# Swapped query halves and a 72-column transpose of the diagonal block

## The chip, the core and the metric

The kernel runs on one core of one Trainium2 chip. The metric is the device time of one execution in microseconds (us). Times of single instructions are given in nanoseconds (ns). TensorE does the matrix products and, by a product with an identity, the transposes; VectorE (DVE), ScalarE (ACT) and GpSimd (POOL) do elementwise work; SyncE (SP) issues the DMAs.

## What is computed

```python
def _attn_ref(q, k, v, s):                      # q, k, v: 4 x 8 x 576 x 64, s: 4 x 8 x 576
    scores = scale * np.matmul(q, k.transpose(0, 1, 3, 2))
    causal = np.triu(np.ones((S, S), dtype=bool), k=1)
    cum = np.cumsum(np.maximum(s, 0.0), axis=-1)
    bias = -(cum[:, :, :, None] - cum[:, :, None, :])
    scores = np.where(causal, -1000000000.0, scores + np.minimum(bias, 0.0))
    attn = softmax(scores)                       # with 1e-9 added to the sum
    return np.matmul(attn, v)

def _moe_ref(x, domain_probs, w1, w2):           # x: 2304 x 512, w1: 4 x 512 x 1024, w2: 4 x 1024 x 512
    p = domain_probs / (domain_probs.sum(-1, keepdims=True) + 1e-09)
    for e in range(4):
        out += p[:, e:e + 1] * (np.maximum(x @ w1[e], 0.0) @ w2[e])
```

The attention of 32 heads is causal; its output, with the heads side by side, goes through a mixture of four experts.

## The kernel before

The program has two stages. In the first, some 270 us long, the attention is computed head by head, and the first expert's products on row groups (lines 945 and 960) are put between as filling for TensorE. In the second, products of the other experts run back to back (line 1302).

**Visits and tiles.** The first eight heads are visited twice with float32 products (lines 745 and 844), the other 24 once, in visits that the code calls `joint`. A joint visit has four tiles of 128 query rows, m = 1 to 4; tile m holds the query rows from 128m - 64 to 128m + 63 (`rows(m)`). The keys lie in blocks of 128. So a tile's rows meet m + 1 key blocks, and its last block, the diagonal one, has entries above zero for the second half of the tile's rows alone: its keys begin at 128m, and the causal mask takes the first 64 rows away.

**A tile's way.** TensorE writes scores into a PSUM bank `S` (line 748, two products with 128 and 68 rows of weights). VectorE adds the mask, takes the extreme and writes the tile `a` to SBUF (line 759, `mask`). ScalarE takes the exponential (767), the sum is inverted (773, 775), the tile is scaled (line 461, called from 780). TensorE transposes the tile block by block into a PSUM bank `T` (line 794); the bank is evicted as a high part on ScalarE (line 466) and a low part on VectorE (line 823). Last come the products with V (line 844). For a key block n those use only query columns from 128n on, so of the diagonal block's transpose only the last 64 columns are used.

**The transpose.** In `nc.tensor.transpose(out, in_, identity)` the tile's block (128 rows by 128 key columns) is the stationary operand that is loaded as weights, and the identity is what is moved, with as many columns as rows come out transposed. There are 456 of them: 336 in the joint visits (2 + 3 + 4 + 5 blocks in each of 24), and 96 of these are of diagonal blocks.

**Order.** Each step is a task with engines, a cost and a priority. A planner, `Sched.run`, walks a model of time and gives each engine its instructions in the order in which the model frees them. All DMAs go through SP's one queue, in that order. The bias parts of the scores come from a DRAM array `ce_d`, written by `emit_ced` (lines 525 to 528) at about 50 us, and read by each joint visit's key and query DMAs (lines 706 to 715) and by `pair_rows` (line 587).

Of the kernel before, what the change touches and what calls it, by code (L numbers as in the profile page):

```python
# [11 lines left out]
F32 = mybir.dt.float32  # L12
F32R = mybir.dt.float32r
AF = mybir.ActivationFunctionType
ALU = mybir.AluOpType
# [38 lines left out]

def rows(m):
    return (0, 64) if m == 0 else (128 * m - 64, 128 * m + 64)
# [48 lines left out]
T_LAG = 200  # L105
S_LAG = 50
# [229 lines left out]
def body(ctx, tc, qk, qkv0, vp, s, dp, w1, w1s, w2, w2s, out):  # L336
# [13 lines left out]
    idn = apool.tile([P, P], F32, name="idn")  # L350
    mask = apool.tile([P, 448 + P], F32, name="mask")
# [88 lines left out]
    ce_d = dram.tile([BH, 6, S], F32R, name="ce_d")  # L440
# [48 lines left out]
    for _ in range(NWARM):  # L489
        nc.tensor.matmul(mo[1], ones_bf[:, 0:128], ones_bf, start=True, stop=True)  # L490
# [5 lines left out]
    make_identity(nc, idn)  # L496
    nc.gpsimd.memset(mask, 0.0)
    nc.gpsimd.affine_select(out=mask[:, 448:], in_=mask[:, 448:], pattern=[[-1, P]], base=0, channel_multiplier=1, compare_op=ALU.is_ge, fill=-8e9)
# [36 lines left out]
    t_ced = sch.add({"SP": 1500}, emit_ced, [t_clo], prio=T_CE, give=[("KK", "ce")], xfer=6 * BH * S * 4)  # L535
# [13 lines left out]
    def emit_mask0(e):  # L549
        hi(e, mask0, mask[:, 448:])  # L550
        nc.gpsimd.memset(mask0[64:P, 0:64], -8e9)
# [8 lines left out]
    def pair_rows(j, h, base):  # L560
# [24 lines left out]
        def f(e):  # L585
            for x, c in ((384, 0), (0, 2)):
                nc.sync.dma_start(out=pair_tile(k)[0:4, x:x + P].bitcast(F32).rearrange("p (y n) -> p y n", y=2),
                                  in_=ced[h - 1:h + 1, c:c + 4, 0:64].rearrange("y r n -> r y n"))
# [28 lines left out]
        tt = sch.add({"PE": t_pe(P)}, lambda e: nc.tensor.transpose(tok["T", (k, "p")][:, 0:P], tok["a0", k], idn), [nm], prio=pr - PT,  # L617
# [36 lines left out]
    for j, (h, ms) in enumerate(VISITS):  # L654
# [40 lines left out]
        else:  # L695
            if pq:
                qk_ready = [ld, ldc]
            else:
# [7 lines left out]
                def f(e, j=j, h=h, ext=ext):  # L706
                    nc.sync.dma_start(out=tok["KK", j][0:64, :, 0:ext].bitcast(F32), in_=AB(j)[64:128, 0:1, 0:ext].bitcast(F32).to_broadcast([64, 2, ext]))
                    nc.sync.dma_start(out=tok["KK", j][64:128, 0, 0:ext].bitcast(F32), in_=AB(j)[64:128, 1, 0:ext].bitcast(F32))
                    nc.sync.dma_start(out=tok["KK", j][64:68, 1, 0:ext].bitcast(F32), in_=ced[h, 2:6, 0:ext])
# [6 lines left out]
                qk_ready = [k_dma, q_dma]  # L716
# [12 lines left out]
        for m in ms[1:] if joint else ms:  # L729
# [7 lines left out]
            for pi, (j0, j1) in enumerate(pieces):  # L737
# [18 lines left out]
                def f(e, m=m, n=n, a=a, j0=j0, j1=j1, c=c, pi=pi):  # L756
                    mx = tok["mx", c]
                    z = tok[f"a{m}", c]
                    nc.vector.tensor_tensor_reduce(  # L759
                        out=z[0:n, j0:j1], in0=tok["S", (c, pi)][0:n, 0:j1 - j0], in1=mask[0:n, 448 - a + j0:448 - a + j1], scale=-0.125,  # L760
# [24 lines left out]
            for pi, blocks in enumerate(tp):  # L785
# [4 lines left out]
                def f(e, m=m, j=j, blocks=blocks, c=c, pi=pi, first=first):  # L790
# [226 lines left out]
    sch.watch = cx_users + [t_ced, t_chi, t_clo, t_cum3]  # L1017
# [521 lines left out]
```

## Time and profile before

| | before |
|---|---|
| time, median of 3 runs | 914.52 us (914.31 to 915.73) |
| profiled execution, time | 914.74 us |
| profiled execution, span | 913.0 us |
| TensorE busy | 905.0 us, 99% of the span |
| VectorE, ScalarE, GpSimd busy | 77%, 55%, 55% |
| granted TensorE clock, mean | 0.999 |

The span reaches from the first to the last instruction; 1.74 us of the profiled execution lie around it. A matmul's recorded time is longer than the pace at which matmuls follow each other, since they are pipelined: the pace is read from one start to the next, and where the engine changes from one kind of product to another, over a few of them.

### The profile page before, as it was taken

The page shows a single profiled execution, that of the slowest core. Times are in us where ns is not written, and L with a number is a line of the kernel's source. Part 1 is how long each engine was busy: PE and PEld are TensorE (multiplying, and loading weights), DVE is VectorE, ACT ScalarE, POOL GpSimd, SP SyncE. Part 2 cuts the span into 40 slices and gives each one's busy share as a digit, 9 for nine tenths or more (in the row PEclk, how much of TensorE's full clock was granted, in tenths as well). Part 3 has the DMA queues.
Part 4 walks back from the last instruction along what each step waited for, and adds up shares of the span by engine and source line. Part 5 has one row for each costly group of instructions (what it writes and reads, how often), then busy time and mean ns, then how long its engine had stood idle before and what let it go on. Part 6 is the DMA issues. An engine that isn't in the chain of part 4 may idle for free.

```text
span 913.0 us, 16499 instructions
## 1 busy us (share of the span) xinstructions
PE 905.0 (99%) x5566; PEld 879.2 (96%) x5566; DVE 705.6 (77%) x1599; ACT 501.3 (55%) x1129; POOL 506.4 (55%) x528
## 2 busy tenths in 40 slices
PE   9999999999999999999999999999999999999998
PEld 6789999899999999999999999999999999999998
DVE  6878787888861854888787788788877887787886
ACT  6898999999972334435343533444244534444343
POOL 4688787887744891055344624471366317451655
PEclk9999999999999999999999999999999999999999
DMA  6788887879626996984786468746775667756201
GB/s 165 197 246 236 225 229 219 250 194 255 181 94 221 392 382 239 357 286 173 264 286 207 161 219 303 243 158 218 252 260 200 204 215 253 256 205 220 70 18 69
DMA packets 101279, 201.34 MB, mean 221 GB/s; under 512 B 11256, under 2 KB 66620, under 8 KB 101196
## 3 DMA queue, kind: packets, MB, share of 16 engines
q1 hardware_dynamic: 101196, 200.30, 67.2%
q8 instruction: 44, 0.72, 0.3%
q14 instruction: 39, 0.32, 0.1%
HBM read 157.34 MB, written 29.05 MB: 204 GB/s over the span
## 4 chain that ended last, share of the span: by engine, by line
PE 91%; ACT 4%; DVE 2%; POOL 1%; issue 1%; DMA 1%; SPq 0%; ACTq 0%; POOLq 0%
PE pb L1302 52%; PE mo L1302 9%; PE mo L945 6%; PE mo L960 5%; PE pv L844 4%; PE pb L960 3%; PE T L794 3%; PE S L748 2%; PE pb L945 2%; PE S L745 2%; ACT a L767 1%; PE X L794 1%; ACT aTh L466 1%; DMA AB_r<-AB_r 1%; DVE aTl L823 1%
## 5 line engine op out<-in xcount | busy, mean ns | idle before, releaser
L1302 PE MATMUL pb<-x,w1h 128*128 128x384 f32 x1064 | 270.7, 335 | 0.0
L1302 PEld LDWEIGHTS pb<-x,w1h 128*128 128x128 f32 x1064 | 191.5, 188 | 2.0 <-ACT t L1335 1.5
L1302 PE MATMUL pb<-x,w1l 128*128 128x384 f32 x532 | 177.8, 334 | 0.0
L1310 ACT ACTIVATE pb<-pb 128x384 f32<-128x384 f32 x112 | 53.2, 475 | 200.5 <-DVE t L1342 111.8
L453 POOL TENSOR_TENSOR hT_r<-t,hT_r 128x768 fp32r<-128x768 f32 x18 | 34.3, 1903 | 167.8 <-PE pb L1302 139.4
L1302 PE MATMUL pb<-hT_r,w2h 128*128 128x384 f32 x432 | 109.7, 334 | 0.0
L1302 PEld LDWEIGHTS pb<-x,w1l 128*128 128x128 f32 x532 | 99.9, 188 | 0.0
L466 ACT ACTIVATE hT_r<-t 128x768 fp32r<-128x768 f32 x76 | 64.0, 843 | 47.3 <-PE pb L1302 44.3
L767 ACT ACTIVATE a<-a,mx 128x576 f32<-128x576 f32 (+4 forms) x136 | 81.0, 597 | 12.8 <-DVE mx L759 9.6
L1425 DVE TENSOR_TENSOR acc<-pb,acc 128x384 f32<-128x384 f32 x152 | 78.5, 549 | 9.6 <-ACT pb L1310 6.1
L945 PE MATMUL mo<-xg,w1h 128*128 128x384 f32 (+1 forms) x304 | 78.3, 327 | 0.0
L1302 PEld LDWEIGHTS pb<-hT_r,w2h 128*128 128x128 f32 x432 | 78.0, 188 | 0.0
L453 DVE TENSOR_TENSOR hT_r<-t,hT_r 128x768 fp32r<-128x768 f32 x58 | 59.8, 1031 | 23.2 <-ACT hT_r L466 22.7
L461 POOL TENSOR_SCALAR a<-a,sm 128x576 f32<-128x576 f32 (+5 forms) x111 | 60.5, 552 | 28.6 <-DVE sm L775 15.0
L1302 PE MATMUL pb<-xg,w2h 128*128 128x384 f32 x288 | 73.3, 335 | 0.0
L1302 PE MATMUL pb<-hT_r,w2l 128*128 128x384 f32 x216 | 72.2, 334 | 0.0
L1342 DVE TENSOR_TENSOR t<-pb,t 128x384 f32<-128x384 f32 x78 | 39.8, 551 | 38.5 <-ACT t L1335 25.6
L453 POOL TENSOR_TENSOR xg<-t,xg 128x768 fp32r<-128x768 f32 x19 | 42.9, 2259 | 40.8 <-ACT xg L466 40.8
L1070 DVE TENSOR_TENSOR t<-t 128x768 f32<-128x768 f32 (+1 forms) x42 | 65.1, 1555 | 0.1
L823 DVE TENSOR_TENSOR aTl<-T,aTh 128x256 fp32r<-128x256 f32 (+2 forms) x103 | 51.2, 508 | 4.6 <-ACT aTh L466 3.5
L759 DVE CUSTOM_DVE_ANT_0 a<-S,mask 128x448 f32<-128x448 f32 (+4 forms) x107 | 48.1, 456 | 7.5 <-PE S L745 6.1
L945 PEld LDWEIGHTS mo<-xg,w1h 128*128 128x128 f32 x304 | 52.1, 190 | 1.4 <-issue 0.7
(245 smaller groups left out, 2331.1 us busy)
## 6 DMA issues: line engine op xcount, KB each, us to landing
x<-xs_d SPq DMA_DIRECT2D x68, 768.0 KB
x<-x_d SPq DMA_DIRECT2D x55, 768.0 KB
xs_d<-x SPq DMA_DIRECT2D x12, 768.0 KB
osb<-p_d SPq DMA_DIRECT2D x19, 384.0 KB
w1r<-in_w1s_dram SPq DMA_DIRECT2D x7, 1024.0 KB
w2r<-in_w2s_dram SPq DMA_DIRECT2D x7, 1024.0 KB
KK<-AB_r SPq DMA_DIRECT2D x24, 288.0 KB
xg<-x_d SPq DMA_DIRECT2D x16, 384.0 KB
```

Of the source, the lines that this page charges most:

```text
L453: (nc.gpsimd if e == "POOL" else nc.vector).tensor_tensor(out=out, in0=in0, in1=in1, op=ALU.subtract)
L461: (nc.gpsimd if e == "POOL" else nc.vector).tensor_scalar(out, in_, scale, 1.0 if bias is None else bias, op0=ALU.mult, op1=ALU.mult if bi ...
L466: nc.scalar.activation(out, in_, AF.Copy)
L759: nc.vector.tensor_tensor_reduce(out=z[0:n, j0:j1], in0=tok["S", (c, pi)][0:n, 0:j1 - j0], in1=mask[0:n, 448 - a + j0:448 - a + j1], scale ...
L767: nc.scalar.activation(z[0:n, 0:bb], z[0:n, 0:bb], AF.Exp, bias=tok["mx", c][0:n, k:k + 1], scale=-1.0, accum_out=tok["sm", c][0:n])
L823: nc.vector.tensor_tensor(out=dst, in0=src, in1=h_.bitcast(F32), op=ALU.subtract)
L945: nc.tensor.matmul(t[:, 0:w], wl[q][:, dc, o:o + P], xgt[:, l, dc, 0:w], start=(u == 0), stop=(u == 3 * KD - 1))
L960: nc.tensor.matmul(t[:, 0:w], wl[fc // 2][:, fc % 2, 128 * dt:128 * dt + 128], ht[:, fc, 0:w], start=(u == 0), stop=(u == 3 * len(fcs) - 1))
L1070: (nc.gpsimd if e == "POOL" else nc.vector).tensor_tensor(out=out, in0=in0, in1=in1, op=op)
L1302: nc.tensor.matmul(ts[u], wv[wl][:, k, 128 * u:128 * u + 128], x[xl_][:, k, :], start=start and k == 0 and n == 0, stop=k == 1 and n == 2, ...
L1310: nc.scalar.activation(out[u], in_[u], AF.Copy)
L1425: nc.vector.tensor_tensor(out=d, in0=ts[u], in1=d, op=ALU.add)
```

## The change

For the 24 heads of the joint visits the host lays the query rows of each tile with their halves swapped: first the rows from 128m, then those from 128m - 64. The diagonal block then has entries above zero in partitions 0 to 63. Its transpose takes partitions 0 to 71 of the tile as stationary operand and moves 72 columns of a small matrix `diag`, into columns 56 to 127 of the block's place in `T`; what stands in columns 0 to 55 isn't read by the products. The other blocks are transposed by an identity whose halves are swapped (`idn`, 64 columns wider), so that the queries leave in their own order. The diagonal block comes first in each task.

The mask has a second copy with swapped halves (`maskx`), and `ce_d` has two more rows: the query side's bias parts are swapped too, which four DMAs of pieces of 64 elements write. `maskx`, the added columns of `idn`, and `diag` are filled by DMAs of their own. In all SP issues 10 DMAs more: `ce_d` takes 8 where it took 3, and `maskx`, `idn` and `diag` 5. The seven products that open the program (line 490) go to different banks.

```diff
+T_HALF = 43
+DG = 72
+T_TURN = 58000
+T_ONES = 45000
+P_TURN = 12500
+P_CED = 12500
...
-    idn = apool.tile([P, P], F32, name="idn")
-    mask = apool.tile([P, 448 + P], F32, name="mask")
+    idn = apool.tile([P, P + 64], F32, name="idn")
+    diag = apool.tile([P, DG], F32, name="diag")
+    mask = apool.tile([P, ZW + P], F32, name="mask")
+    maskx = apool.tile([P, ZW + P], F32, name="maskx")
...
     def emit_ced(e):
-        nc.sync.dma_start(out=ced[:, 0:2], in_=cx[:, 0:1].to_broadcast([BH, 2, S]))
-        nc.sync.dma_start(out=ced[:, 2:4], in_=tok["KK", "ce"][0:BH].bitcast(F32))
-        nc.sync.dma_start(out=ced[:, 4:6], in_=cx[:, 3:4].to_broadcast([BH, 2, S]))
+        ce = tok["KK", "ce"][0:BH].bitcast(F32)
+        nc.sync.dma_start(out=ced[:, 4:6], in_=ce)
+        nc.sync.dma_start(out=ced[:, 2:4, 0:64], in_=ce[:, :, 0:64])
+        for l in range(2):
+            new, old = (t[:, l, 64:S].rearrange("h (m x n) -> h m x n", x=2, n=64) for t in (ced[:, 2:4], ce))
+            for x in range(2):
+                nc.sync.dma_start(out=new[:, :, x], in_=old[:, :, 1 - x])
...
+    t_ones = turn_of(T_ONES, (ced[:, 0:2], cx[:, 0:1].to_broadcast([BH, 2, S])), (ced[:, 6:8], cx[:, 3:4].to_broadcast([BH, 2, S])), xfer=300000)
+    turn_of(T_TURN, (maskx[0:64], mask[64:P]), (maskx[64:P], mask[0:64]), xfer=230000)
+    t_turn = turn_of(T_TURN, (idn[:, P:P + 64], idn[:, 0:64]), (diag[0:DG, 0:DG - 64], idn[0:DG, 64:DG]), (diag[0:DG, DG - 64:DG], idn[0:DG, 0:64]), xfer=80000)
+    t_ced = sch.add({"SP": 2900}, emit_ced, [t_clo, t_ones], prio=P_CED, give=[("KK", "ce")], xfer=4 * BH * S * 4)
...
-                    for k, x in enumerate(blocks[::-1] if not first and tok["par", j] else blocks):
-                        nc.tensor.transpose(t[:, 128 * k:128 * k + 128], z[:, 128 * x:128 * x + 128], idn)
-                tt = sch.add({"PE": t_pe(128) * len(blocks)}, f, [nm, prev, par], prio=pr - PT, take=[("T", (c, pi))],
+                    order = list(enumerate(blocks[::-1] if not first and tok["par", j] else blocks))
+                    for k, x in sorted(order, key=lambda y: joint and y[1] != m):
+                        if joint and x == m:
+                            nc.tensor.transpose(t[:, 128 * k + 128 - DG:128 * k + 128], z[0:DG, 128 * x:128 * x + 128], diag[0:DG])
+                        else:
+                            nc.tensor.transpose(t[:, 128 * k:128 * k + 128], z[:, 128 * x:128 * x + 128], idn[:, 64:64 + P] if joint else idn[:, 0:P])
+                tt = sch.add({"PE": t_pe(128) * len(blocks) - T_HALF * (joint and blocks[-1] == m)}, f, [nm, prev, par], prio=pr - PT, take=[("T", (c, pi))],
...
+    turn = np.concatenate([np.arange(64), np.arange(64, S).reshape(-1, 2, 64)[:, ::-1].reshape(-1)])
+    qx = np.concatenate([q[:NH], q[NH:, turn]])
```

The planner's numbers move the order from about 46 us on. On TensorE, in one of the first joint visits, a tile with four key blocks (m = 3) stood like this before; `X_101`, `S_96` and `S_97` are PSUM banks, `a_1_126` is the tile, `pv_100` the product with V of the visit before, `KK_111` the keys:

```order
L844 MATMUL pv_100<-aTl,V_115 128x320
L844 MATMUL pv_100<-aTl,V_115 128x192
L794 MATMUL X_101<-idn,a_1_126 128x128 x4
L748 MATMUL S_96<-KK_111,AB_r 128x288 x2
L945 MATMUL mo_103<-xg,w1l_83 128x256
L945 MATMUL mo_103<-xg,w1h_79 128x256
```

and stands like this now (`a_1_128` is that tile, `a_1_126` the tile ahead of it, m = 2; line 824 is the diagonal block's transpose, 826 the others', 775 the scores):

```order
L876 MATMUL pv_102<-aTl,V_117 128x192
L824 MATMUL X_103<-diag,a_1_126 128x72
L826 MATMUL X_103<-idn,a_1_126 128x128 x2
L824 MATMUL T_101<-diag,a_1_128 128x72
L826 MATMUL T_101<-idn,a_1_128 128x128 x3
L775 MATMUL S_99<-KK_113,AB_r 128x320 x2
```

In each group of transposes the first one is narrow, and another transpose always follows it. Over the whole program the number of TensorE's instructions is the same, 96 transposes have 72 columns and 360 have 128; ahead of the last product of the attention stand 626 of the filling products where 633 stood, and ahead of the first joint scores stand 401 products where 386 stood.

On SP, where the bias array is written, the queue stood like this before (`ce_d` is the bias array, `AB_f` and `raw` are loads of heads, `x_d` stores of attention output):

```order
L676 DMA AB_f<-in_qk_dram 64x576
L677 DMA AB_f<-in_qk_dram 64x256
L686 DMA AB_f<-cx 2x1x1152
L526 DMA ce_d<-cx 32x2x576
L527 DMA ce_d<-KK_110 32x1152
L528 DMA ce_d<-cx 32x2x576
L680 DMA raw_104<-in_qk_dram 128x576
L682 DMA vraw_114<-in_vp_dram 128x320
```

and stands like this now, up to a few rows ahead of the first joint visit's key DMA (line 734):

```order
L539 DMA ce_d<-KK_112 32x1152
L540 DMA ce_d<-KK_112 32x2x64
L544 DMA ce_d<-KK_112 32x4x64 x4
L927 DMA x_d<-xh_134 128x2x256
L707 DMA raw_107<-in_qk_dram 128x576
L927 DMA x_d<-xg 128x2x320
L554 DMA maskx<-mask 64x448 x2
L554 DMA idn<-idn 128x64
L554 DMA diag<-idn 72x8
L554 DMA diag<-idn 72x64
```

The two DMAs for the constant parts of `ce_d` now stand earlier, ahead of the last float32 visit's loads; the other six stand where three stood, and five fills more stand between these and the first joint visit's keys.

## Rows read from the trace of the kernel before

**Rows 1.** The page's first lines: span, then busy time and share by engine.
```profile
span 913.0 us, 16499 instructions
PE 905.0 (99%) x5566; PEld 879.2 (96%) x5566; DVE 705.6 (77%) x1599; ACT 501.3 (55%) x1129; POOL 506.4 (55%) x528
```
**Rows 2.** Busy time by stretch; x is the number of instructions, sum and clock behind.
```profile
core 0: us, PE busy (x) PEld busy (x) DVE busy (x) ACT busy (x) POOL busy (x), PEclk, DMA share, GB/s
...
150.00:200.00 50.00, 48.62 (x330) 44.71 (x328) 41.73 (x165) 47.60 (x132) 41.34 (x75) 1.00 0.82 224
200.00:250.00 50.00, 50.00 (x333) 47.31 (x334) 41.39 (x166) 45.32 (x128) 38.67 (x70) 1.00 0.74 211
...
500.00:600.00 100.00, 100.00 (x577) 99.62 (x577) 78.92 (x121) 42.86 (x76) 47.89 (x29) 1.00 0.65 224
```
**Rows 3.** Whom TensorE waited for: us in total, times, longest us.
```profile
PE T L633 <- DVE aTl L823: 0.9, 1, 0.9
PE S L745 <- DMA AB_f<-cx: 0.8, 1, 0.8
```
**Rows 4.** Line 794, the transposes: ns min/median/max, first and last start; loads, then products.
```profile
L794 PEld LDWEIGHTS T<-idn,a x326: 137/141/198, 9.5 to 268.1; 128*128 128x128 f32 x163
L794 PE MATMUL T<-idn,a x326: 270/272/331, 9.7 to 268.2; 128*128 128x128 f32 x163
```
**Rows 5.** Weight loads of lines 945 and 745, in the same view.
```profile
L945 PEld LDWEIGHTS mo<-xg,w1h x304: 186/189/245, 20.2 to 341.0; 128*128 128x128 f32 x152
...
L745 PEld LDWEIGHTS S<-AB_f x66: 186/190/198, 6.6 to 64.7; 66*128 66x128 f32 x66
```
**Rows 6.** TensorE in order of time around two ordinary 128-column products: start us, us.
```profile
110.45 0.22 PE L594 MATMUL S<-stage_r 128*128 128x128 f32 x1
110.51 0.28 PE L595 MATMUL S<-stage_r 128*128 128x128 f32 x1
110.62 0.33 PE L945 MATMUL mo<-xg,w1h 128*128 128x256 f32 x1
110.79 0.36 PE L748 MATMUL X<-KK,AB_r 128*128 128x192 f32 x2
```
**Rows 7.** TensorE in order of time around two transposes, then around nine.
```profile
120.72 0.28 PE L945 MATMUL mo<-xg,w1l 128*128 128x256 f32 x1
120.84 0.28 PE L945 MATMUL mo<-xg,w1h 128*128 128x256 f32 x1
120.96 0.38 PE L794 MATMUL T<-idn,a 128*128 128x128 f32 x2
121.10 0.36 PE L945 MATMUL mo<-xg,w1h 128*128 128x256 f32 x1
121.30 0.28 PE L945 MATMUL mo<-xg,w1l 128*128 128x256 f32 x1
...
131.59 0.82 PE L794 MATMUL T<-idn,a 128*128 128x128 f32 x6
132.24 0.49 PE L794 MATMUL X<-idn,a 128*128 128x128 f32 x3
```
**Rows 8.** SP's issues in order of time, 48 to 70 us: start us, us.
```profile
48.12 0.51 SPq L676 DMA_DIRECT2D AB_f<-in_qk_dram  x1
...
50.52 0.35 SPq L527 DMA_DIRECT2D ce_d<-KK  x1
...
61.39 0.56 SPq L709 DMA_DIRECT2D KK<-ce_d  x1
...
69.92 0.49 SPq L714 DMA_DIRECT2D AB_r<-ce_d  x1
```
**Rows 9.** Line 748, scores of the joint visits: ns min/median/max, first and last start.
```profile
L748 PE MATMUL S<-KK,AB_r x204: 250/309/452, 73.6 to 259.9; 128*128 128x288 f32 x39, 128*128 128x320 f32 x22, 128*128 128x192 f32 x21, 128*128 128x448 f32 x20
```

More of the change, by code (lines that the diff above doesn't have):

```diff
@@ L439, in body @@
     mask0 = apool.tile([P, P], F32, name="mask0")
-    ce_d = dram.tile([BH, 6, S], F32R, name="ce_d")
+    ce_d = dram.tile([BH, 8, S], F32R, name="ce_d")
     ced = ce_d.bitcast(F32)
@@ L487, in keep_warm @@
         return 110
-    for _ in range(NWARM):
-        nc.tensor.matmul(mo[1], ones_bf[:, 0:128], ones_bf, start=True, stop=True)
+    warmed = [b[1] for p in ("X", "T", "S") for b in sch.pools[p]] + mo
+    for i in range(NWARM):
+        nc.tensor.matmul(warmed[i], ones_bf[:, 0:128], ones_bf, start=True, stop=True)
     nc.vector.memset(warm, 0.0)
@@ L534, in body, with turn_of, f @@
     t_cum2.both = True
-    t_ced = sch.add({"SP": 1500}, emit_ced, [t_clo], prio=T_CE, give=[("KK", "ce")], xfer=6 * BH * S * 4)
+    def turn_of(at, *pairs, xfer):
+        def f(e):
+            for o, i in pairs:
+                nc.sync.dma_start(out=o, in_=i)
+        t = sch.add({"SP": 500 * len(pairs)}, f, prio=P_TURN, xfer=xfer, seq="turn")
+        t.ready = at
+        return t
+    t_ones = turn_of(T_ONES, (ced[:, 0:2], cx[:, 0:1].to_broadcast([BH, 2, S])), (ced[:, 6:8], cx[:, 3:4].to_broadcast([BH, 2, S])), xfer=300000)
+    turn_of(T_TURN, (maskx[0:64], mask[64:P]), (maskx[64:P], mask[0:64]), xfer=230000)
+    t_turn = turn_of(T_TURN, (idn[:, P:P + 64], idn[:, 0:64]), (diag[0:DG, 0:DG - 64], idn[0:DG, 64:DG]), (diag[0:DG, DG - 64:DG], idn[0:DG, 0:64]), xfer=80000)
+    t_ced = sch.add({"SP": 2900}, emit_ced, [t_clo, t_ones], prio=P_CED, give=[("KK", "ce")], xfer=4 * BH * S * 4)
     PR = NT // 64
@@ L549, in emit_mask0 @@
     def emit_mask0(e):
-        hi(e, mask0, mask[:, 448:])
+        hi(e, mask0, mask[:, ZW:])
         nc.gpsimd.memset(mask0[64:P, 0:64], -8e9)
@@ L585, in f @@
         def f(e):
-            for x, c in ((384, 0), (0, 2)):
+            for x, c in ((384, 0), (0, 4)):
                 nc.sync.dma_start(out=pair_tile(k)[0:4, x:x + P].bitcast(F32).rearrange("p (y n) -> p y n", y=2),
@@ L616, in pair_rows @@
         nm.both = True
[L617 removed]
+        tt = sch.add({"PE": t_pe(P)}, lambda e: nc.tensor.transpose(tok["T", (k, "p")][:, 0:P], tok["a0", k], idn[:, 0:P]), [nm], prio=pr - PT,
                      take=[("T", (k, "p"))], give=[("a0", k)])
@@ L754, in body, with f @@
                 firstq.setdefault(j, qt)
-                def f(e, m=m, n=n, a=a, j0=j0, j1=j1, c=c, pi=pi):
+                def f(e, m=m, n=n, a=a, j0=j0, j1=j1, c=c, pi=pi, joint=joint):
                     mx = tok["mx", c]
                     z = tok[f"a{m}", c]
+                    w0 = 0 if j1 <= a else ZW - a + j0
                     nc.vector.tensor_tensor_reduce(
-                        out=z[0:n, j0:j1], in0=tok["S", (c, pi)][0:n, 0:j1 - j0], in1=mask[0:n, 448 - a + j0:448 - a + j1], scale=-0.125,
+                        out=z[0:n, j0:j1], in0=tok["S", (c, pi)][0:n, 0:j1 - j0], in1=(maskx if joint else mask)[0:n, w0:w0 + j1 - j0], scale=-0.125,
                         scalar=1e30 if pi == 0 else mx[0:n, 0:1], op0=ALU.add, op1=ALU.min, accum_out=mx[0:n, pi:pi + 1])
```

15 lines of the change are left out of this document (8 added, 7 removed).

## The prediction

> **What bounds the kernel now.** I read the page's first lines, then busy time by stretch, then whom TensorE waited for, and last single products in order of time. TensorE is busy for 905.0 of 913.0 us [rows 1]. In the dense second stage it takes 577 products of 384 columns in 100 us, one each 173 ns, at granted clock 1.00, the 2.4 GHz level [rows 2]. In the attention stage the others are near their limits too (from 150 to 250 us ScalarE is busy for 92.9 of 100 us, VectorE for 83.1), but TensorE loses 1.4 us in the one half of that stretch and nothing in the other [rows 2], and its longest waits for others that the view names are 0.9 and 0.8 us [rows 3]. Filling products stand in its queue between the steps of the attention. So TensorE's own work sets the time, through both stages: a nanosecond taken from its work is a nanosecond of the span, as long as the new order brings no new waits.
>
> **What a transpose costs now.** The recorded durations (272 ns [rows 4]) overlap, so the pace is what counts. Six transposes start from 131.59 to 132.24 us: 108 ns each [rows 7]. In a group of two, 0.34 us pass from the first transpose (120.96) to the second product behind the pair (121.30); one product of 256 columns, which has a pace of 0.12 us (120.72 to 120.84), is in that, and 0.22 us are left for two transposes, 110 ns each [rows 7]. I take 109 ns.
>
> What sets these 109 ns decides the case. Two things could: the 128 columns moved, or the load of the next product's weights, which goes on meanwhile. For ordinary products the price of columns follows from two rows: 173 ns at 384 columns [rows 2] and 120 ns at 256 [rows 7] give 0.42 ns a column (one clock at 2.4 GHz) and some 13 ns fixed. By that, 128 columns would take 67 ns. But two ordinary products of 128 columns take, from 110.45 to 110.79 us less the 0.12 us of the 256-column product between, 0.22 us, 110 ns each [rows 6]: there the next weights set the pace. These loads are recorded with 189 ns, and with 190 ns where only 66 rows are loaded [rows 5]: fewer rows don't make a load shorter. So if a transpose's 109 ns were also the next load, the change would bring nothing, since the load of a tile's block still has 128 columns.
>
> The transposes' own loads, however, are recorded with 141 ns [rows 4], 48 ns less than the ordinary 189 [rows 5]. If an ordinary load holds the array for 110 of its 189 ns, and the other 79 are overlap, a transpose's load holds it for about 62 ns. That doesn't explain 109. The columns do, if a float32 transpose takes two clocks for each: 128 x 0.84 = 107 ns. This is an inference from two recorded durations; no transpose with fewer columns stands in this trace.
>
> **The rule that speaks against it.** By the Trainium skill (TensorE: Matmul & The Clock Gate, LDWEIGHTS), the time of a weight load goes by its columns and not by its rows, some 107 ns for 128 columns by the page's formula. The ordinary products of [rows 6] and the 66-row loads of [rows 5] agree with that; the transposes' shorter loads in [rows 4] don't. By the page alone the sum below would be 0; it is the first rival.
>
> **The narrow transpose.** With 72 columns at 109/128 = 0.85 ns it would take 61 ns; with 13 ns fixed and the rest by columns, (109 - 13) x 72/128 + 13 = 67 ns. The next transpose's load (about 62 ns) fits under either. I take 66, near the upper of the two, because load and columns then end almost together. The bounds are wider: 109 at the one end (nothing saved, as the ordinary products of [rows 6] would have it), 61 at the other; less than 61 is excluded, since neither load nor columns get shorter than that by these rows. The order matters here: the narrow one comes first in its group, so that a transpose's short load follows it. Ahead of an ordinary product it would wait for a 110 ns load, and save nothing.
>
> So 24 visits x 4 tiles = 96 narrow transposes save 43 ns each (42 to 48), **4.1 us** (4.0 to 4.6). The row count of 72 changes nothing, by the 66-row loads.
>
> **The other parts.** *Wide transposes* with the halves swapped move 128 columns as before: 0. *Mask copy*: VectorE reads as many elements from `maskx` as from `mask`: 0. *Evictions* still read whole 128-column blocks: 0. *Opening products* on other banks, seven as before: 0. *Ten DMAs more on SP*: from 48.12 to 61.39 us SP issues 19 DMAs, one each 0.74 us with their waits [rows 8]; ten cost it up to 7.4 us. They move, by their shapes, some 0.43 MB, which at 224 GB/s [rows 2] are 2 us of the DMA engines. Behind them in SP's one queue are the first joint visit's keys (61.39 us before) and queries (69.92) [rows 8], and for these TensorE's first line-748 product waits, at 73.6 us [rows 9]. The 12 us between 61.39 and 73.6 cover it: TensorE has float32 visits and filling to do, and the new order holds the first joint scores back by 15 products. I cost it at 0; with the cover gone it is 7.4 us. *The new order*: 626 filling products, not 633, stand ahead of the attention's last product, and the rest follow later; no work is added, so 0 by itself. Its waits are drawn anew, though. From 150 to 200 us TensorE lost 1.4 us, from 200 to 250 none [rows 2]; the stage has four such stretches, so a luckier order gives back up to 1.4 us, and one with 1.4 us in each costs 4.2.
>
> **Sum.** The profiled execution took 914.74 us, its span 913.0 and 1.74 around it. 914.74 - 4.1 = 910.6. The median of the three runs is 914.52, 0.2 lower; against it I expect 910.4, and put **910.5**.
>
> **Rivals.**
> *The next load sets the pace (12 in 100).* For: two ordinary products show just this floor, 110 ns [rows 6], and 109 is close to it. Against: the transposes' loads are 48 ns shorter in the records [rows 4, 5]. The change then moves fewer columns without a gain: 914.7.
> *A load that waits for the columns ahead of it (6 in 100).* If the transpose's load (about 55) and its 128 columns at one clock (53) followed each other instead of overlapping, that would give 108 too; 56 columns less at 0.42 ns would save 23 ns each, 2.2 us: 912.4. Against: the ordinary loads overlap.
> *The new order waits (8 in 100).* ScalarE's 92.9 of 100 us [rows 2] leave 7 us in 100; a stage some 4 us shorter leaves 5. If every stretch of 50 us then loses the 1.4 us of the worst, 4.2 us come back: 914.8, and between 912.7 and 914.8 if some do.
> *SP's queue (6 in 100), the slower side.* If the ten DMAs delay the first joint keys and queries past the moment when TensorE has used up what stands ahead of the first scores, it waits there in order with everything behind it. It decides from the point where SP is more than 12 us late, less what the queries' DMA already takes of that (they are issued at 69.92, 3.7 us ahead of the scores): so possible from about 4 us. Fully uncovered it costs 7.4 us: 914.7 - 4.1 + 7.4 = 918.0.
>
> **How the numbers follow.** The forecast has 68 in 100; its own range is 908.9 (4.6 us, and 1.0 fewer waits) to 912.3 (4.0, and 1.8 more). About 0.2%, 1.8 us, is what a measurement of this kernel can tell from no change; that is below 912.7 and above 916.3. Faster: 68, most of the partial rival and a little of the order's: 74. Same: the load's rival, the order's rest and a part of SP's: 20. Slower: 6. The range for 8 in 10 has to reach over the two rivals at 914.7 and 914.8 in part: 908.8 to 914.8.
>
> **What would show it.** Right: in the trace after, a narrow transpose is followed by the next transpose 61 to 67 ns later, and wide ones still by 109; TensorE's instructions are as many, and the span is near 908.8. The attention's last transpose comes about 4 us before 268.2 [rows 4]. Wrong: the narrow one's pace is 109, with the load of the next starting or ending later; or the pace is 66 and TensorE's waits from 70 to 270 us have grown, on ScalarE or VectorE; or there is a wait of some us ahead of the first line-775 product, on a DMA of keys or queries.

## The result and the profile after

The change makes the kernel slower: 921.62 us (median of four runs, 920.6 to 923.32) against 914.42 for before on the same chip, a ratio of 1.0077 with a 95% interval of 1.0059 to 1.0095. The forecast was 910.5, with a range up to 914.8. The profiled execution took 920.6 us, its span is 918.8.

The page's first lines of after, in the form of [rows 1]: TensorE counts as many instructions as before, and it is again busy for 99%.

```profile
span 918.8 us, 16532 instructions
PE 906.3 (99%) x5566; PEld 877.3 (95%) x5566; DVE 704.6 (77%) x1599; ACT 498.7 (54%) x1127; POOL 509.1 (55%) x530
```

**The narrow transpose does what was forecast.** TensorE in order of time, after (start us, us): each narrow transpose (83.08, 83.26) is followed by a wide one 60 ns later, and the wide one of 83.14 by the next transpose 120 ns later; over all of them the medians are 66 and 109 ns.

```profile
83.08 0.23 PE L824 MATMUL T<-diag,a 72*128 72x72 f32 x1
83.14 0.28 PE L826 MATMUL T<-idn,a 128*128 128x128 f32 x1
83.26 0.23 PE L824 MATMUL T<-diag,a 72*128 72x72 f32 x1
83.32 0.38 PE L826 MATMUL T<-idn,a 128*128 128x128 f32 x2
```

Line 824 in after (ns min/median/max, first and last start): the product is recorded 45 ns shorter than in [rows 4], the load no longer and no shorter than there, though it loads 72 rows.

```profile
L824 PEld LDWEIGHTS T<-diag,a x66: 137/140/146, 83.0 to 265.8; 72*128 72x128 f32 x66
L824 PE MATMUL T<-diag,a x66: 226/227/271, 83.1 to 266.0; 72*128 72x72 f32 x66
```

But the attention hardly ends earlier. The prediction wanted its last transpose some 4 us ahead of 268.2 us [rows 4]; in after the last one into `T` starts at 268.1:

```profile
L826 PE MATMUL T<-idn,a x247: 270/273/329, 9.7 to 268.1; 128*128 128x128 f32 x124
```

**Where the time went.** Busy time by stretch, after and then before (columns as in [rows 2]). TensorE loses 0.6 to 1.8 us in each of the three stretches behind 70 us (before 0, 0 and 0.7), and 1.9 us between 330 and 340 us; in the 10 us after that its granted clock is 0.83.

```profile
70.00:80.00 10.00, 9.38 (x76) 8.93 (x76) 7.16 (x28) 8.28 (x24) 8.05 (x12) 1.00 0.84 218
80.00:90.00 10.00, 9.21 (x70) 8.33 (x69) 8.31 (x37) 9.31 (x29) 8.51 (x20) 1.00 0.95 253
90.00:100.00 10.00, 8.24 (x60) 7.31 (x60) 7.78 (x34) 9.53 (x26) 8.69 (x15) 1.00 0.91 253
...
330.00:340.00 10.00, 8.10 (x45) 7.78 (x45) 7.17 (x8) 3.85 (x6) 9.84 (x6) 1.00 1.11 349
340.00:350.00 10.00, 9.13 (x40) 8.21 (x41) 1.12 (x2) 2.12 (x4) 5.29 (x3) 0.83 0.86 344
```
```profile
70.00:80.00 10.00, 10.00 (x86) 9.85 (x84) 7.73 (x28) 8.80 (x23) 8.57 (x14) 1.00 0.73 202
80.00:90.00 10.00, 10.00 (x79) 9.51 (x78) 8.38 (x40) 8.80 (x29) 8.09 (x17) 1.00 0.94 264
90.00:100.00 10.00, 9.32 (x72) 8.85 (x70) 8.33 (x33) 9.39 (x27) 8.63 (x16) 1.00 1.04 233
...
330.00:340.00 10.00, 10.00 (x60) 10.00 (x59) 9.45 (x8) 4.24 (x7) 10.00 (x5) 1.00 1.09 358
340.00:350.00 10.00, 9.94 (x58) 9.62 (x57) 4.55 (x8) 3.97 (x8) 6.14 (x4) 1.00 0.97 373
```

Whom TensorE waited for, after (us in total, times, longest): two DMAs lead the list, where [rows 3] had nothing above 0.9.

```profile
PE mo L977 <- DMA xg<-x_d: 2.7, 3, 2.3
PE S L775 <- DMA AB_r<-AB_r: 1.1, 1, 1.1
```

Busy time hides short waits, since recorded durations overlap. So I also counted by starts: a product's pace is taken as 0.42 ns a column and 13 ns, 173 at 384 columns, at least 110 (float32 attention products twice the columns, a wide transpose 109, a narrow one 66), and what lies between two starts beyond the pace of the first I call **waits**; a fall of the clock counts among them. These are worked out, not read. Before and after differ thus, in us:

| | work at pace | waits 70 to 100 | 100 to 280 | 320 to 360 | elsewhere |
|---|---|---|---|---|---|
| before | 893.8 | 1.5 | 6.4 | 0.7 | 6.2 |
| after | 889.6 | 5.5 | 7.3 | 5.9 | 6.1 |

The 4.2 us of work are gone, and 10.0 us of waits have come: 5.8 us more between the spans of the two profiled executions (the medians are 7.2 apart).

**Waits for queries.** Two of the waits between 70 and 100 us end with a DMA that brings queries. SP and then TensorE in order of time, after:

```profile
71.03 0.98 SPq L740 DMA_DIRECT2D AB_r<-AB_r  x1
...
76.33 0.45 PE L775 MATMUL S<-KK,AB_r 128*128 128x192 f32 x2 [0.57 <-issue]
...
93.06 0.44 PE L775 MATMUL S<-KK,AB_r 128*128 128x192 f32 x2 [1.12 <-DMA AB_r<-AB_r]
```

At 76.33 stand the first joint scores. The view names no releaser there (`issue`), but the trace's record of semaphores does: the last piece of the DMA issued at 71.03 lands at 76.24 us, and TensorE goes on right behind it. In before the same DMA was issued at 69.39 and had landed at 71.68, 2.0 us ahead of the first joint scores:

```profile
69.39 0.48 SPq L713 DMA_DIRECT2D AB_r<-AB_r  x1
```

**The wait at 338 us.** SP's issues in order of time, after and then before: the four loads `xg` of the expert stage's input stand behind five loads of `acc` (partial sums, read back from DRAM) in after, and ahead of them in before.

```profile
326.01 7.63 SPq L1244 DMA_DIRECT2D acc<-o_d  x5
333.74 2.72 SPq L967 DMA_DIRECT2D xg<-x_d  x4
```
```profile
327.22 1.94 SPq L935 DMA_DIRECT2D xg<-x_d  x4
...
329.72 8.08 SPq L1212 DMA_DIRECT2D acc<-o_d  x5
```

TensorE then, after: it stands idle for 2.26 us, and a product of 384 columns, 173 ns in [rows 2], has a pace of 320 ns some 4 us later (344.26 to 344.58).

```profile
340.39 0.61 PE L977 MATMUL mo<-xg,w1h 128*128 128x384 f32 x2 [2.26 <-DMA xg<-x_d]
...
344.26 0.52 PE L977 MATMUL mo<-xg,w1l 128*128 128x384 f32 x1
344.58 0.84 PE L977 MATMUL mo<-xg,w1h 128*128 128x384 f32 x2
```

The two groups of DMAs are put in by the planner in different ways: the `xg` loads follow the fillings, the `acc` loads come when a sum of the planned costs of the expert products reaches a constant, `T_BACK`, 50.0. In the new order seven fillings more come behind the attention, the sum reaches the constant ahead of the `xg` loads, and the two groups change places. This is read from the planner's code; the next two runs test it.

### The profile page after: what moved, and what is told of

It reads as the page before. It is cut to its first block, busy times and chain, and to the rows that moved or that the text cites. A ratio compares the mean times of both kernels' runs of the same rounds, so it can differ in the third digit from the quotient of the medians.

```text
span 918.8 us, 16532 instructions
## 1 busy us (share of the span) xinstructions
PE 906.3 (99%) x5566; PEld 877.3 (95%) x5566; DVE 704.6 (77%) x1599; ACT 498.7 (54%) x1127; POOL 509.1 (55%) x530
## 4 chain that ended last, share of the span: by engine, by line
PE 91%; ACT 2%; DMA 2%; DVE 2%; issue 1%; POOL 1%; SPq 0%; POOLq 0%; ACTq 0%; DVEq 0%
PE pb L1334 52%; PE mo L1334 9%; PE mo L977 6%; PE mo L992 5%; PE pv L876 4%; PE S L775 3%; PE pb L992 2%; PE T L826 2%; PE pb L977 2%; PE S L772 1%; PE X L826 1%; DMA xg<-x_d 1%; DMA KK<-AB_r 1%; ACT a L795 1%; PE X L775 1%
## 5 line engine op out<-in xcount | busy, mean ns | idle before, releaser
L795 ACT ACTIVATE a<-a,mx 128x448 f32<-128x448 f32 (+4 forms) x136 | 81.2, 599 | 11.9 <-DVE mx L787 8.0
L977 PE MATMUL mo<-xg,w1h 128*128 128x384 f32 (+1 forms) x296 | 75.0, 331 | 2.9 <-DMA xg<-x_d 2.7
L472 POOL TENSOR_SCALAR a<-a,sm 128x448 f32<-128x448 f32 (+5 forms) x110 | 61.6, 564 | 26.0 <-DVE sm L803 13.1
L1334 PEld LDWEIGHTS pb<-xg,w2h 128*128 128x128 f32 x288 | 51.9, 188 | 0.3 <-ACT pb L1342 0.2
```

The lines of the kernel that those rows point to most:

```text
L472: (nc.gpsimd if e == "POOL" else nc.vector).tensor_scalar(out, in_, scale, 1.0 if bias is None else bias, op0=ALU.mult, op1=ALU.mult if bi ...
L795: nc.scalar.activation(z[0:n, 0:bb], z[0:n, 0:bb], AF.Exp, bias=tok["mx", c][0:n, k:k + 1], scale=-1.0, accum_out=tok["sm", c][0:n])
L977: nc.tensor.matmul(t[:, 0:w], wl[q][:, dc, o:o + P], xgt[:, l, dc, 0:w], start=(u == 0), stop=(u == 3 * KD - 1))
L1334: nc.tensor.matmul(ts[u], wv[wl][:, k, 128 * u:128 * u + 128], x[xl_][:, k, :], start=start and k == 0 and n == 0, stop=k == 1 and n == 2, ...
```

## The experiments

The theory after this reading: the narrow transpose saves its 4.1 us, and three things take more than that back: the changed places of `xg` and `acc`, the added DMAs on SP, and something in the attention stage. The rivals: that the narrow transpose itself brings no gain, or that the new order as a whole costs the time.

### Which DMAs come first: e1_back, e4_before_back

In after the constant is raised, so that the `xg` loads go first again; in before it is lowered, so that they go last.

```diff
-T_BACK = 50.0
+T_BACK = 51.5      # e1_back, in after
+T_BACK = 49.0      # e4_before_back, in before
```

> The changed kernel with one number, T_BACK, at 51.5 instead of 50.0. It moves five large loads (acc from o_d) on SP behind the four loads of xg for the last row group, as they stood before the change; nothing else moves on any engine. If the order of these loads is what makes TensorE wait at 338 us and lose its clock after it, that wait goes and the time falls by the 5.2 us that are lost between 320 and 360 us: 915.3 (914.5 to 916.5). If the DMA engines are simply full there, whatever the order, the wait stays and the time is 920 to 922.

> The kernel before with T_BACK at 49.0 instead of 50.0: on SP the five loads of acc and one of x change places with the four of xg, nothing else moves. If the order of these loads is the cause, the kernel before gets the same wait and the same fall of the clock without any narrow transpose: 919.5 (917.5 to 921.5). If the cause lies in the changed attention stage, it stays at 914.5.

e1_back took 917.16 us (in brackets here and below: ratio to before on the same chip, and its 95% interval; 1.0026, 1.0016 to 1.0035), 4.5 less than after, but more than the 914.5 to 916.5 expected. e4_before_back took 919.15 (1.005, 1.0031 to 1.0069), 4.8 more than before and within its range, and shows the same wait and the same fall of the clock:

```profile
PE mo L945 <- DMA xg<-x_d: 2.0, 2, 1.8
...
340.00:350.00 10.00, 9.74 (x48) 8.98 (x47) 1.32 (x3) 2.21 (x4) 5.18 (x3) 0.83 0.68 263
```

So the places of two groups of DMAs cost some 4.5 us, in either kernel. In after 2.7 us of it are the wait, and about 1.7 the lower clock behind it (0.83 for 10 us). The other 2.7 us of after's loss are elsewhere. A part of what e1_back keeps over before is a fall of the clock that after's profile doesn't have: between 90 and 100 us, with waits for queries in front of it (e1_back: whom TensorE waited for, then busy time by stretch).

```profile
PE S L775 <- DMA AB_r<-AB_r: 1.5, 2, 1.0
...
90.00:100.00 10.00, 8.40 (x50) 7.47 (x50) 7.82 (x33) 9.22 (x26) 8.50 (x14) 0.83 0.87 251
```

### Narrow against wide in the new order: e2_wide, e6_wide_back

The same order on every engine, and the diagonal block transposed with 128 columns like the others; e2_wide is after with this edit, e6_wide_back is e1_back with it.

```diff
-    nc.tensor.transpose(t[:, 128 * k + 128 - DG:128 * k + 128], z[0:DG, 128 * x:128 * x + 128], diag[0:DG])
+    nc.tensor.transpose(t[:, 128 * k:128 * k + 128], z[:, 128 * x:128 * x + 128], idn[:, 64:64 + P])
```

> The changed kernel with all 128 columns and rows moved for the diagonal blocks too, by the same permutation as the others; the order on every engine is that of the changed kernel, instruction for instruction. If a narrow transpose saves 43 ns and each is on the path, this is 96 x 43 ns = 4.1 us slower than the changed kernel: 925.7. If the attention stage's waits on other engines have taken the saving, the wide ones fill these waits and it is less than 1.5 us slower: under 923.

> The changed kernel with wide transposes for the diagonal blocks and with T_BACK at 51.5: e1_back's order on every engine, with 128 columns moved where e1_back moves 72. Against e1_back (917.2) it shows what the narrow transposes are worth in an otherwise equal program. If every nanosecond of them is on the path: 921.3. If waits on other engines take part of it, as the waits of e2_wide between 100 and 280 us suggest (4.6 us where the changed kernel has 7.3): 918.7 (918 to 919.5).

e2_wide took 924.26 us, 2.6 more than after and between its two cases, but its `xg` wait is also longer (3.3 us), so the pair doesn't tell what the narrow one is worth. e6_wide_back took 917.81 (916.8 to 918.1), only 0.65 more than e1_back (915.96 to 919.55), though its work at pace is 4.2 us more. e1_back's waits from 100 to 280 us are 6.6, e6_wide_back's 3.9. Most of the saving turns into waits, as the second case had it.

### The start of the added DMAs: e3_early

```diff
-T_TURN = 58000
-T_ONES = 45000
+T_TURN = 20000
+T_ONES = 20000
```

> The changed kernel with T_TURN and T_ONES at 20000: the fills of maskx, idn and diag and the constant rows of ce_d stand about ten places earlier on SP, so that six extra DMAs and not eleven lie ahead of the first joint visit's keys; the planner's order changes with it, and the xg loads again stand ahead of the acc loads. If SP's queue causes the 3 us of TensorE's waits between 70 and 100 us, they fall to 1 us or less, and with the wait at 338 us gone too the time is 911 to 913.5. If these waits come from the tighter plan of the other engines, they stay at about 3 us: 914.5 to 916.

It took 923.32 us (1.0087, 1.0069 to 1.0105), far above both cases. The planner drew the order anew: the first joint scores come at 79.4 us, and `hT_r` and `xg` waits of 1.8 and 1.5 us head TensorE's list. It says nothing on SP's queue alone, and was a poor experiment, because the edit changed more than the queue. The next ones hold the order fixed.

### The added DMAs alone, in the order of before: e5_before_dmas, e10_turns, e10_fills

Ten DMAs of the change's shapes (the mask copies 320 columns wide and not 448), into memory that nothing reads, are issued behind `ce_d`'s three; the planner doesn't know of them, so every engine keeps the order of before. e10_turns has the five turned rows of `ce_d` alone, e10_fills the five fills alone.

```diff
         nc.sync.dma_start(out=ced[:, 4:6], in_=cx[:, 3:4].to_broadcast([BH, 2, S]))
+        nc.sync.dma_start(out=ced[:, 6:8, 0:64], in_=ce[:, :, 0:64])
+        ...                                     # four pieces of 64 elements, as in after
+        for p, q in ((0, 64), (64, 0)):
+            nc.sync.dma_start(out=maskx[p:p + 64], in_=mask[q:q + 64, 128:448])
+        nc.sync.dma_start(out=idx, in_=idn[:, 0:64])
+        nc.sync.dma_start(out=diag[0:72, 0:8], in_=idn[0:72, 64:72])
+        nc.sync.dma_start(out=diag[0:72, 8:72], in_=idn[0:72, 0:64])
```

> The kernel before with ten DMAs more on SP, unread by anything, right behind its three writes of ce_d: the turned copies of the bias parts and the five fills (the mask copies 320 columns wide). The planner knows nothing of them, so TensorE, VectorE, ScalarE and GpSimd keep the order of before, instruction for instruction. If SP's queue causes the 4 us of TensorE's waits that the change adds between 70 and 100 us, they come here too: 917 to 919. If the planner's new order causes them, the time stays at 914.4 (914 to 915.5).

> e5_before_dmas with the five turned writes of ce_d alone, four of them in pieces of 64 elements. If SP's cost goes by the number of DMAs: 917.8 (916.5 to 919), as e10_fills. If small pieces cost most of it: 919.5 to 921.

> e5_before_dmas with the five fills alone (two mask copies of 64 partitions, three identity pieces) behind the three of ce_d; the order of before elsewhere. If SP's cost goes by the number of DMAs: half of e5_before_dmas's 7 us, 917.8 (916.5 to 919). If the many small pieces of the turned bias writes cost most of it, 915 or less.

All ten: 921.36 us (1.0068, 1.0055 to 1.0081), 7.1 more than before and above the range expected. The two halves: 915.14 for the turned rows (1.0, 0.9991 to 1.0009) and 916.42 for the fills (1.001, 1.0001 to 1.002), and neither of the two cases held. The price isn't a sum: five DMAs cost nothing that can be told or 1 to 2 us, ten cost 7.1. e5's trace shows why. The chain of waits in order of time (start us, us, what; only its main pieces): SP issues the added DMAs until 58.18, then the `raw` load of a head, which lands at 61.22.

```profile
54.20 0.52 SPq L539
...
56.94 1.24 SPq L542
58.18 0.04 issue
58.23 2.99 DMA raw<-in_qk_dram
...
61.30 0.13 ACT AB_r L469
...
62.28 0.42 DVE hT_r L965
62.71 0.34 DVE aTl L837
```

In before that load is issued right behind the three DMAs of `ce_d`, 6.9 us sooner, and ScalarE reads `raw` at 58.64 without a wait (SP, then ScalarE in order of time):

```profile
51.38 0.42 SPq L680 DMA_DIRECT2D raw<-in_qk_dram  x1
...
58.64 0.67 ACT L466 ACTIVATE AB_r<-raw 128x576 fp32r<-128x576 f32 x1
```

From 51.38 to 58.64 are 7.3 us, and the load takes 3.0 in e5; so by these rows, as an estimate, it could come some 4.3 us later at no cost, and ten DMAs make it 6.9.

ScalarE in order of time in e5: the instruction that reads `raw` waits 2.32 us, and behind it on the same engine stand the evictions `aTh` (high parts) of an earlier tile. VectorE's low parts `aTl` follow them, and TensorE waits for these (ScalarE, then TensorE).

```profile
61.30 0.68 ACT L469 ACTIVATE AB_r<-raw 128x576 fp32r<-128x576 f32 x1 [2.32 <-DMA raw<-in_qk_dram]
61.89 0.36 ACT L962 ACTIVATE hT_r<-mo 128x256 fp32r<-128x256 f32 x1
62.15 0.76 ACT L469 ACTIVATE aTh<-T 128x256 fp32r<-128x256 f32 x2
...
63.10 0.44 PE L808 MATMUL T<-idn,a 128*128 128x128 f32 x2 [2.19 <-DVE aTl L837]
```

Busy time by stretch in e5: TensorE loses 2.2 us, and the granted clock is 0.74 and 0.75 for 20 us.

```profile
60.00:70.00 10.00, 7.81 (x33) 6.01 (x32) 5.27 (x19) 7.83 (x19) 6.29 (x10) 0.74 1.02 340
70.00:80.00 10.00, 10.00 (x66) 9.71 (x66) 5.49 (x18) 5.78 (x17) 6.05 (x11) 0.75 0.75 206
```

So the stop is 2.2 us of the 7.1, and the lower clock some 5 (0.26 and 0.25 of 10 us). One of e5's six runs kept its clock and took 918.2.

The profiled execution of e10_fills, the slowest of its eleven (921.09 us), has the same picture: TensorE busy for 8.41 of the first 10 us, clock 0.71 and 0.78. There the load is issued at 55.30, only 3.9 us later than in before, but takes 5.5 us to land; so not the queue alone decides, but also how long the load itself takes. The other ten runs took 915.6 to 917.71, which leaves no room for a loss of that size. So with five fills the load seems to come in time in most runs (none of these is traced), and with ten it does not.

### Fewer DMAs in the new order: e7_pool_masks

In e1_back the five fills are replaced by instructions of GpSimd early in the program.

```diff
-    turn_of(T_TURN, (maskx[0:64], mask[64:P]), (maskx[64:P], mask[0:64]), xfer=230000)
-    t_turn = turn_of(T_TURN, (idn[:, P:P + 64], idn[:, 0:64]), ...
+    def emit_turn(e):
+        hi(e, idn[:, P:P + 64], idn[:, 0:64])
+        hi(e, diag[0:DG, 0:DG - 64], idn[0:DG, 64:DG])
+        hi(e, diag[0:DG, DG - 64:DG], idn[0:DG, 0:64])
+        nc.gpsimd.memset(maskx, 0.0)
+        for p, b in ((0, 64), (64, 0)):
+            nc.gpsimd.affine_select(out=maskx[p:p + 64, ZW:], ...)
+    t_turn = sch.add({"POOL": 2200}, emit_turn, prio=6500)
```

> The changed kernel with maskx, the added columns of idn and diag made by GpSimd at the start and not by DMAs, and T_BACK at 51.5; five DMAs fewer ahead of the first joint visit. If SP's queue causes the waits between 70 and 100 us they fall to about 2 us: 912 to 914. If the new order does, the planner having moved everything again, they are as likely to be more as to be less: 914 to 919.

It took 914.34 us (0.9998, 0.999 to 1.0007), 2.8 less than e1_back and no different from before. Between 70 and 100 us TensorE no longer waits for a DMA (its waits that the view names, 1.1, 0.6 and 0.5 us, are for VectorE), and the clock stays up:

```profile
90.00:100.00 10.00, 8.71 (x63) 7.69 (x63) 8.37 (x34) 9.66 (x26) 9.24 (x15) 1.00 0.87 236
```

Its work is 4.2 us less than before's; its waits from 70 to 100 us are still 5.0 (before 1.5), from 100 to 280 us 5.9 (6.4). Here the narrow transposes' saving is not lost in the attention stage as a whole, but 3.5 us go at the stage's beginning. What causes these stays open. The planner has drawn the order anew, against e1_back too, so what the five fills alone cost is only read, not tested.

### The whole change in the order of before: e8_same_order, e9_lean, e11_lean_wide

e8 has the whole change, with the planner kept from seeing it. e9 also drops nine of the ten DMAs: GpSimd makes the masks at the start, and VectorE turns the bias rows with three copies. e11 is e9 with wide transposes (the edit of e2_wide).

```diff
-T_HALF = 43
+T_HALF = 0                                     # e8 and e9: the planner counts as before
...
+    nc.gpsimd.memset(maskx, 0.0)               # e9: masks by GpSimd at the start
...
+        turned = cx_all[BH:2 * BH, 0:2]
+        nc.vector.tensor_copy(turned[:, :, 0:64], ce[:, :, 0:64])
         for l in range(2):
+            new, old = (t[:, l, 64:S].rearrange("h (m x n) -> h m x n", x=2, n=64) for t in (turned, ce))
+            nc.vector.tensor_copy(new, old[:, :, ::-1])
+        nc.sync.dma_start(out=ced[:, 2:4], in_=turned)
```

> The whole change with the order of before: the planner is told the old costs and tasks (T_HALF 0, one task for ce_d, no task for the fills), and the ten DMAs are issued behind the three of ce_d as in e5_before_dmas. VectorE, ScalarE and GpSimd have the order of before; TensorE too, but that the narrow transpose leads its group. T_BACK at 50.0 leaves the xg loads ahead of the acc loads, as before. If the loss came from the planner's new order alone: 914.4 - 4.1 = 910.3 with all of the narrow transposes' saving on the path, 912.8 with 1.5 us of it. If SP's queue costs 3 to 4 us, the time is 914 to 917, and e5_before_dmas shows the same cost.

> The whole change with the order of before, as e8_same_order, but with one DMA more than before instead of ten: GpSimd makes maskx, the added identity columns and diag at the start, and VectorE turns the bias parts in three copies ahead of one DMA. If the ten DMAs are what cost e5_before_dmas 7 us, nothing of that is left, and the time is that of before less what the narrow transposes are worth: 913.0 with the 1.3 us that e8_same_order has over e5_before_dmas, 910.2 with all 4.1 us. If the turned layout costs something else, it stays at 915 or above.

> e9_lean with wide transposes for the diagonal blocks: the control for the narrow ones without the queue's loss. If the attention stage is paced by the other engines between its steps, 1 us slower than e9_lean: 914.0. If TensorE paces it once the queue is free, 4.1 us slower: 914.3 against 910.2. Either way the turned layout by itself should cost nothing against before (914.3).

e8 took 920.1 us (1.0055, 1.0043 to 1.0067), above the 914 to 917 expected, and 1.3 less than e5, which has the same DMAs and wide transposes. e9 took 915.84 (1.0004, 0.9995 to 1.0013) and e11 915.56 (1.0006, 0.9998 to 1.0015). Against my expectation, the narrow transposes bring nothing here that the medians can tell, with SP's queue and the order out of the way. Waits from 100 to 280 us are 11.3 in e9 and 7.1 in e11: the whole saving. About 1.7 us of e9's are a fall of the clock (0.83 from 165 to 175 us), which its profiled execution shows and six of its eleven runs don't; the runs of both with a mean clock of 0.999 or more have medians of 914.78 and 915.43, so up to 0.65 us of the 4.2 may be left. That e11 lies 0.95 us above before by medians is not clear of noise. Busy time there, e9 and then e11: ScalarE is busy for 89 and 90%, and it is TensorE that loses.

```profile
100.00:280.00 180.00, 177.34 (x1230) 166.46 (x1230) 143.38 (x552) 160.92 (x443) 131.86 (x233) 0.99 0.71 198
```
```profile
100.00:280.00 180.00, 178.49 (x1234) 168.77 (x1233) 143.51 (x553) 161.45 (x442) 132.43 (x234) 1.00 0.71 199
```

### Is it ScalarE? e12 to e15

e12 and e13 are e9 and e11 with the exponential of half of each tile's columns, e14 and e15 with that of 64 columns. The instructions and their order stay; these four leave the rest of the exponential out, to lighten ScalarE alone.

```diff
-                nc.scalar.activation(z[0:n, 0:bb], z[0:n, 0:bb], AF.Exp, ...
+                nc.scalar.activation(z[0:n, x0:bb], z[0:n, x0:bb], AF.Exp, ...    # x0 = bb // 2, then bb - 64
```

> The kernel of e9_lean (narrow diagonal transposes, the order of before, one extra DMA) with one thing left out: in the joint visits ScalarE takes the exponential of the second half of each tile's columns only, so the instruction stands in the same place and the rest of the tile stays as VectorE wrote it. ScalarE is busy for about 161 of 180 us from 100 to 280 us in e9_lean; this should fall by some 15 to 20 us. Theory A, ScalarE's pace in the attention stage eats the narrow transposes' saving: with ScalarE lighter, TensorE's own work sets the time, the waits from 100 to 280 us fall from 11.3 us to under 7, and the time is 910 to 912 us. Theory B, VectorE or the length of the tile's chain does it: the waits stay at 10 to 11 us and the time at 914.5 to 916 us.

> The same with all transposes 128 columns wide (e11_lean_wide with the exponential of the second half of each tile's columns only). Theory A: its waits from 100 to 280 us, 7.1 us in e11_lean_wide, fall less, since TensorE's own work was already the longer; the time is 913.5 to 915.5 us, 3 to 4 us above e12_narrow_light. Theory B: 914.5 to 916 us, within 0.7 us of e12_narrow_light.

> As e12_narrow_light, but ScalarE takes the exponential of only the last 64 columns of each tile in the joint visits (the rest of the tile is left as VectorE wrote it). In e12_narrow_light ScalarE was still busy for 46 of 50 us from 150 to 200 us, since the stage ran faster. Theory A, ScalarE is the only one that sets the pace: TensorE's waits from 100 to 280 us (11.3 us in e9_lean, 5.0 in e12_narrow_light) fall to 2 us or less and the time to 905 to 907 us. Theory B, ScalarE sets it together with VectorE and GpSimd (both busy for 80 to 87% there): the waits stay at 4 to 5 us and the time at 907.5 to 909 us.

> The same with all transposes 128 columns wide. Theory A: 909 to 910.5 us, 3 to 4 us above e14_narrow_least. Theory B: 909 to 910.5 us, at most 2 us above it.

| exponential of | narrow, us | wide, us | narrow less wide | waits 100 to 280, narrow / wide |
|---|---|---|---|---|
| all columns (e9, e11) | 915.84 | 915.56 | +0.3 | 11.3 / 7.1 |
| half (e12, e13) | 909.01 | 910.77 | -1.8 | 5.0 / 2.9 |
| 64 columns (e14, e15) | 907.61 | 910.44 | -2.8 | 3.2 / 2.5 |

The three pairs ran on three chips, where before took 914.61, 915.58 and 914.73; within a pair the chip is the same. Busy time in e14 and then e15:

```profile
100.00:280.00 180.00, 179.19 (x1275) 173.68 (x1274) 144.00 (x552) 141.99 (x440) 131.53 (x232) 1.00 0.72 207
```
```profile
100.00:280.00 180.00, 179.38 (x1259) 174.01 (x1259) 144.97 (x552) 142.31 (x441) 131.47 (x232) 1.00 0.71 202
```

The lighter ScalarE's work, the more of the saving is seen, from nothing (0.65 in the runs at full clock) to 2.8 of some 4.2 us, and both kernels gain 5 to 8 us. The ranges of e12 and e13 touch (908.22 to 910.87, 910.54 to 911.67), those of e14 and e15 don't (906.83 to 908.61, 910.13 to 911.27). So, in the order of before, ScalarE's load in the attention stage takes at least half of what the narrow transposes save: 3.1 of 4.2 us by medians, 2.2 against the runs at full clock, come out when it is made lighter. In after's own order the same loss shows (e1_back against e6_wide_back), but ScalarE wasn't lightened there. Neither theory's numbers held in full: e12 and e13 came out below them, e14's time is in theory B's range and its waits lie between the two. Lightening ScalarE shortens each tile's own chain too, from scores to transposes; whether it is the engine's total load or this latency that counts, these runs don't part. What takes the rest (1.4 us, by these medians) stays open; VectorE, busy for 80% of the stretch, wasn't lightened.

## Why the prediction was wrong

**The narrow transpose at 66 ns: right.** After shows it followed by the next transpose 60 to 70 ns later. Two clocks for a column fit that nearly: 56 columns fewer take 43 ns less, 0.77 each, and two clocks at the 2.4 GHz level are 0.83. The rival that the next load sets the pace (12 in 100) falls, as does the one of a load that waits for the columns, which allowed 23 ns (and reckoned a load at 55 that stood at 62 before). The Trainium skill (TensorE: Matmul & The Clock Gate, LDWEIGHTS) puts 128 columns of weights at some 107 ns; the trace disagrees for these transposes, whose next load has 128 columns and lets them follow at 66. The 96 of them save 4.2 us of work, 4.1 were forecast.

**"TensorE's own work sets the time, through both stages": this step failed first.** It rested on busy times of 97 and 100% [rows 2] and on a list of waits with nothing above 0.9 us [rows 3]. Both hide what matters here: a product recorded with 272 ns that has a pace of 109 covers a gap of up to 160 ns ahead of the next one. By starts, TensorE waited 6.4 us from 100 to 280 us in before already, and with the narrow transposes in the same order 11.3 (e9). Weight loads, in the same rows, showed more: PEld 44.71 and 47.31 of 50 us in the attention stage, 99.62 of 100 in the second. The Trainium skill (Perfetto Trace Analysis, Identifying the Most-Contended Engine) says that the busy share of matmuls is not a good measure of how near TensorE is to its limit, and names that of weight loads as one to use instead; the runs agree: from 100 to 280 us e9, which waits 11.3 us, has PEld at 166.46 of 180, e15, which waits 2.5, at 174.01, and PE differs by 2.0 alone. ScalarE's 92.9 of 100 us stood in the rows too. I named it in the third rival, priced that rival at up to 4.2 us, and gave it 8 in 100. The waits of e9 and e11 differ by just these 4.2, but that is luck: my price was three stretches at 1.4 us, and not the saving. The rival deserved the larger share. A saving on one engine counts only up to the slack of the next, and ScalarE's 7% of idle time, in a chain, was not slack that could be used in full.

**Ten DMAs on SP at 0: failed.** In the order of before they cost 7.1 us (e5); the rival gave 7.4 for the case without cover, with 6 in 100. That the two are so near is luck, since the price came another way: 2.2 us of a stop and some 5 of a lower clock, which no term of the sum had. I looked for whom the queue delays among the joint visits' keys, 12 us ahead of their use. The first to be late was a load that stands right behind the ten, `raw`, of which I had not asked when it is needed; ScalarE waits for it in order, with evictions behind it, then TensorE for those, and then TensorE's clock falls. In after itself the planner spreads the ten, and this wait is not there. The one that the rival named is, at a smaller size: the first joint scores come at 76.3 us instead of 73.6 [rows 9], TensorE stands idle for 0.57 us ahead of them until the queries land, and for 1.12 us ahead of a later visit's. The 12 us of cover were counted from the keys; the queries, issued 3.7 us ahead of the scores, had only that. These two are 1.7 of the 4.0 us that waits grew by between 70 and 100 us.

**The new order at 0 "by itself": failed, and at the largest price.** That 626 fillings and not 633 stand ahead of the attention's end was in front of me; I called it no work added. By the planner's code the seven that moved carried a sum over a constant that sets when DMAs are issued, 60 us later: 4.5 us (e1_back, e4_before_back). No rival had it, and SP's order at 330 us, which could be compared before the run, was not compared.

By parts, in medians: 4.5 us for `xg` behind `acc` (after less e1_back), and 2.8 more that go when the five fills do (e1_back less e7, each on its own chip and in its own order; some 1.7 of it the clock that falls in e1_back's profile alone). What is left, e7, equals before: its narrow transposes pay for what else the change costs. No version here that does all the work beats before.

## What to carry to other kernels

Ask of each engine how much it can give when another is made faster: here the others in the chain were busy for 73 to 90% of the stage, shortening the one at 99% brought 0 to 0.65 us of 4.2, and the test is to lighten each neighbour once. Judge TensorE by starts and weight loads, not by busy time. After a planner's change compare every queue to its end, also where the diff doesn't reach, and above all the order of DMAs.

## What was not expected of the hardware

A stop of TensorE can cost far more than its length. After an idle stretch of 2.26 us in after the granted clock is 0.83 in the next 10 us, and products of 384 columns follow each other at 320 ns instead of 173, which is the 1.2 GHz level; that is about 1.7 us more. In e5, around an idle stretch of 2.19 us, the mean clock is 0.74 and 0.75 in two stretches of 10 us, some 5 us more. Shorter stops were enough elsewhere: in e9 the clock is 0.83 from 165 to 175 us with idle stretches of 1.02 and 0.20 us in them, while before, which has one of 0.9 us [rows 3], kept 1.00.

Weight loads of a float32 transpose are recorded with 140 ns, whether of 72 or 128 rows, and permit a pace of 66 ns; ordinary loads with as many columns are recorded with 189, and products with 128 columns behind them take 110 [rows 5, 6].

The price of DMAs ahead of a load jumps once the load's cover is used up: with the five fills more the kernel takes 915.6 to 917.71 us and once in eleven runs 921.09, with all ten 918.2 or more in every run of e5 and e8.
